# Ten identity products whose results nobody reads, set between TensorE's first and third groups of scores

## The chip, the cores and the metric

The kernel runs on one core of a Trainium2 chip. A core has five engines that work side by side, each through its own list of instructions in order: TensorE (PE, matrix products; its loads of the stationary operand are listed as PEld), VectorE (DVE), ScalarE (ACT), GpSimd (POOL) and SyncE (SP, which here issues the loads and stores). An engine waits for another through semaphores. SBUF holds the operands, PSUM the results of PE, in banks; a PSUM tile of 512 float32 per partition is one bank. The metric is the time of the whole kernel on the device, in microseconds (us), lower is better.

## What is computed

The first part is an attention with a gated state, for 4 batches of 8 heads, 768 steps and heads of 48:

```python
f = 1 / (1 + exp(-f_logit))
for t in range(S):
    state = f[:, :, t, :, None] * state + einsum('bhd,bhe->bhde', k[:, :, t], v[:, :, t])
    y[:, :, t] = einsum('bhd,bhde->bhe', q[:, :, t], state)
```

Its output x (4 x 768 x 384, the heads side by side) goes through a second part:

```python
theta = x @ w_theta
zr, zi = x * cos(theta), x * sin(theta)
u = x + einsum('ts,bsd->btd', w_tok_r, zr) + einsum('ts,bsd->btd', w_tok_i, zi)
return u + maximum(u @ w_ch, 0)
```

## The kernel before

The time axis is cut into chunks of 128 steps, six for each batch, 24 in all; a chunk has two halves of 64. The gates become sums of logarithms, so that a chunk needs no step-by-step recurrence. For chunk m the steps are, by the two letters that the table `ORDER` uses: loads of f, k, q and v (`lf`, `lk`, `lq`, `lv`); the gates on DVE, ACT and POOL (`gc`, `go`, `gs`, `ge`, `gp`), with `gs` a running sum along time (L298, whose first operand `carry` holds 1, and 0 where a chunk begins) and `ge` two exponentials; the scaling of queries and keys (`gq` L313, `gk` L318). PE then has, in small products of 48 or 64 rows and columns, the scores `sc` (L354, keys times queries), the turn of the keys `ke` (L368, four transposes against the identity `ident`), the state sums `up` (L383, turned keys times v), the products with the old state `qs` (L414) and the output `ou` (L422, scores times v). Between them stand copies by other engines: `kt` copies the turned keys (`ktok`), `ma` masks the scores (L360), `sa`, `st` and `sm` form the middle state and the new state on DVE or POOL (L389 to L399), `xc` copies the output to `x`. The turn of x `xt` (L432, three transposes) and the angles `th` (L463, x times w_theta, three products of 128x128 by 384 columns in the first batch) lead to the second part, whose products over time (`f0` to `f2`, L519, tile `pm`) and over channels (`c`, L537) fill most of the run.

Nothing is scheduled by a machine: the table `ORDER` lists the steps of all chunks in one line of words, a loop at the end of the kernel calls them in that order, and each engine gets its instructions in that order. `sc` at its third occurrence is the scores of the third chunk, and so on; `/P`, `/A` or `/D` behind a word puts a step on POOL, ACT or DVE. PSUM has four single banks, tag `b`, and two pairs, tag `a` (the tiles `wide`); `PLACES` says which place each tile takes in turn.

Before the first step the kernel already runs products that nobody reads: 22 of 128x384 from a tile of ones, `seed`, into the bank `b3` (L624 to L629).

Of the kernel before, what the change touches and what calls it, by code (L numbers as in the profile page):

```python
# [75 lines left out]
}  # L76
ORDER = (
# [37 lines left out]
)  # L115


@with_exitstack
def gla_moe_kernel(
# [480 lines left out]
    def group(fn):  # L600
        return lambda n: fn(n // KD, n % KD)
# [165 lines left out]
```

## Time and profile before

| | |
|---|---|
| time, median of 3 runs | 334.77 us (334.46 to 335.71) |
| profiled execution | 335.46 us, its span 333.8 us |
| PE busy | 320.6 us, 96% of the span |
| PE loads / DVE / ACT / POOL busy | 85% / 73% / 57% / 29% |
| mean granted clock of PE | 0.975 |
| read from memory, written | 40.10 MB, 4.72 MB |

The span runs from the first to the last instruction of the program. Busy PE is the time in which a product was in the array by the profile; products are pipelined and their ends are modelled. The granted clock is the share of its full rate that PE was given in a stretch; it is 1.00 or 0.50 here, and a value between means that a stretch saw both. A product of two float32 operands stands in the trace as two records (16 small products as x32), a transpose as one. Times in the rows are counted from the start of the span.

### The profile page before, as it was taken

The page shows a single profiled execution, that of the slowest core. Times are in us where ns is not written, and L with a number is a line of the kernel's source. Part 1 is how long each engine was busy: PE and PEld are TensorE (multiplying, and loading weights), DVE is VectorE, ACT ScalarE, POOL GpSimd, SP SyncE. Part 2 cuts the span into 40 slices and gives each one's busy share as a digit, 9 for nine tenths or more (in the row PEclk, how much of TensorE's full clock was granted, in tenths as well). Part 3 has the DMA queues.
Part 4 walks back from the last instruction along what each step waited for, and adds up shares of the span by engine and source line. Part 5 has one row for each costly group of instructions (what it writes and reads, how often), then busy time and mean ns, then how long its engine had stood idle before and what let it go on. Part 6 is the DMA issues. An engine that isn't in the chain of part 4 may idle for free.

```text
span 333.8 us, 10065 instructions
## 1 busy us (share of the span) xinstructions
PE 320.6 (96%) x4342; PEld 283.4 (85%) x4342; DVE 244.5 (73%) x418; ACT 190.4 (57%) x315; POOL 97.1 (29%) x96
## 2 busy tenths in 40 slices
PE   6689999999999999999999999999999999999993
PEld 6576676566777889999999999999999999999992
DVE  6997999988998977799896667784677476520231
ACT  6787788884778965775766855691363236200010
POOL 3352404024231408516522352321324110132010
PEclk9956999999999999999999999999999999999998
DMA  7988799695604410604444251371102200000012
GB/s 226 379 299 302 227 404 348 244 349 179 224 2 165 152 57 26 217 15 133 139 139 140 81 176 40 105 223 33 48 2 82 73 26 26 0 2 24 24 49 79
DMA packets 21618, 45.54 MB, mean 136 GB/s; under 512 B 2368, under 2 KB 5440, under 8 KB 21568
## 3 DMA queue, kind: packets, MB, share of 16 engines
q1 hardware_dynamic: 21568, 44.83, 39.9%
q8 instruction: 36, 0.59, 0.7%
q14 instruction: 14, 0.11, 0.1%
HBM read 40.10 MB, written 4.72 MB: 134 GB/s over the span
## 4 chain that ended last, share of the span: by engine, by line
PE 93%; DMA 3%; DVE 2%; issue 1%; ACT 1%; SPq 0%; DVEq 0%
PE pm L519 48%; PE pth L463 13%; PE pch L537 11%; PE wide L422 5%; PE wide L414 4%; PE wide L354 4%; PE pxt L432 3%; PE psk L368 3%; PE wide L383 3%; DMA k<-in_k_dram 2%; DMA f<-in_f_dram 1%; DVE f L298 1%; DVE k L318 0%; DVE ut L551 0%; ACT f L294 0%
## 5 line engine op out<-in xcount | busy, mean ns | idle before, releaser
L519 PE MATMUL pm<-wp,z 128*128 128x384 f32 x648 | 119.9, 338 | 0.0
L519 PEld LDWEIGHTS pm<-wp,z 128*128 128x128 f32 x648 | 112.7, 188 | 0.7
L519 PE MATMUL pm<-value,z 128*128 128x384 f32 x144 | 49.8, 488 | 0.0
L537 PE MATMUL pch<-uhl,wch 128*128 128x384 f32 x216 | 42.1, 342 | 0.0
L523 DVE TENSOR_TENSOR ut<-pm,ut 128x384 f32<-128x384 f32 x24 | 13.2, 551 | 36.4 <-PE pm L519 36.2
L519 PEld LDWEIGHTS pm<-value,z 128*128 128x128 f32 x144 | 26.1, 190 | 14.9
L537 PEld LDWEIGHTS pch<-uhl,wch 128*128 128x128 f32 x216 | 37.5, 188 | 0.8
L298 DVE TENSOR_TENSOR_SCAN f<-carry,f 128x512 f32<-128x512 f32 x24 | 29.9, 1250 | 1.7 <-ACT f L294 1.6
L530 POOL TENSOR_TENSOR uhl<-ut,uhl 128x384 fp32r<-128x384 f32 x13 | 14.0, 1078 | 55.1 <-ACT uhl L182 36.2
L288 POOL TENSOR_SCALAR f<-f 128x512 f32<-128x512 f32 x11 | 19.4, 1764 | 20.1 <-DMA f<-in_f_dram 13.3
L454 POOL TENSOR_TENSOR xl<-ut,xh 128x384 fp32r<-128x384 f32 x9 | 10.1, 1125 | 50.7 <-ACT xh L182 23.8
L182 ACT CAST uhl<-ut 128x384 fp32r<-128x384 f32 x13 | 6.7, 512 | 31.9 <-DVE ut L523 31.9
L182 ACT COPY x<-wide 128x384 f32<-128x384 f32 x22 | 10.5, 477 | 24.2 <-PE wide L422 23.1
L463 PE MATMUL pth<-wth,xh 128*128 128x384 f32 x108 | 22.9, 347 | 0.0
L551 DVE SCALAR_TENSOR_TENSOR ut<-pch,ut 128x384 f32<-128x384 f32 x24 | 13.1, 552 | 12.8 <-PE pch L537 12.8
L309 POOL COPY pes<-p 128x4 f32<-128x4 f32 x24 | 8.7, 362 | 46.0 <-ACT p L305 45.1
L503 POOL TENSOR_TENSOR z<-w,z 128x768 fp32r<-128x768 f32 x7 | 13.5, 1927 | 27.6 <-DVE z L182 16.8
L422 PEld LDWEIGHTS wide<-v,sc 64*64 64x64 f32 x768 | 14.9, 138 | 7.2 <-issue 4.1
L318 DVE SCALAR_TENSOR_TENSOR k<-f,k 128x512 f32<-128x512 f32 x24 | 19.2, 801 | 2.2 <-ACT f L306 1.9
L463 PEld LDWEIGHTS pth<-wth,xh 128*128 128x128 f32 x108 | 19.0, 188 | 1.1
L479 ACT ACTIVATE w<-w 128x384 f32<-128x384 f32 x16 | 8.4, 524 | 19.8 <-DVE w L474 19.8
L496 DVE TENSOR_TENSOR w<-w,x 128x768 f32<-128x768 f32 x18 | 18.0, 997 | 2.3 <-ACT w L487 2.3
(88 smaller groups left out, 619.6 us busy)
## 6 DMA issues: line engine op xcount, KB each, us to landing
v<-in_v_dram SPq DMA_DIRECT2D x24, 384.0 KB, 4.8
f<-in_f_dram SPq DMA_DIRECT2D x24, 256.0 KB, 3.8
q<-in_q_dram SPq DMA_DIRECT2D x24, 256.0 KB, 4.7
k<-in_k_dram SPq DMA_DIRECT2D x24, 256.0 KB, 4.9
raw<-in_w_i_dram SPq DMA_DIRECT2D x12, 384.0 KB, 6.2
raw<-in_w_r_dram SPq DMA_DIRECT2D x12, 383.8 KB, 5.6
out_dram<-ut SPq DMA_DIRECT2D x21, 192.0 KB, 2.2
raw<-in_w_theta_dram SPq DMA_DIRECT2D x2, 383.8 KB, 7.0
```

What stands on the lines that cost most here:

```text
L182: (nc.scalar.copy if on(usual) is nc.scalar else on(usual).tensor_copy)(dst, src)
L288: on(nc.vector).tensor_scalar(ft, ft, F_MIN, None, op0=ALU.max)
L298: nc.vector.tensor_tensor_scan(fl, carry[:, pairs(h)].rearrange("p n t -> p (n t)"), fl, 0.0, ALU.mult, ALU.add)
L318: nc.vector.scalar_tensor_tensor(kt, loaded["f", m][:, pairs(h)], E_TOP, kt, op0=ALU.min, op1=ALU.mult)
L354: nc.tensor.matmul(out[HALF[j ^ t], j, p, :], kt[r, p, HALF[t]], qt[r, p, HALF[t]], start=True, stop=True)
L422: nc.tensor.matmul(out[HALF[t], j, p, :], scs[m][HALF[a], j, p, :], v2[HALF[a], t, p, :], start=(t == 0 and m % NC == 0 and p == 0), stop= ...
L463: nc.tensor.matmul(pths[m], l, r, start=(n == 0), stop=(n == len(ms) - 1))
L496: nc.vector.tensor_tensor(zs[m] if full else w, w, xs[m].unsqueeze(1).to_broadcast([P, 2, DM]), op=ALU.mult)
L503: on(nc.vector).tensor_tensor(zs[m][:, 0], ws[m], zs[m][:, 1], op=ALU.subtract)
L519: nc.tensor.matmul(pms[g, d], l, r, start=(s == 0 and i == 0), stop=(s == NC - 1 and i == len(ms) - 1))
L530: on(nc.vector).tensor_tensor(us[g, d][:, 0], uts[g][:, d, :], us[g, d][:, 1], op=ALU.subtract)
L537: nc.tensor.matmul(pcs[g, d], l, r, start=(es[0] == 0 and n == 0), stop=(es[-1] == KD - 1 and n == len(ms) - 1))
```

## The change

A table `WARM` and a step `wm` are added. Each `wm` is one product of the identity (stationary, 128x128) with the first 512 or 256 columns of `carry` (moving), float32 both, into a bank that the table names, `b3` for the first five and `b1` for the rest. No instruction reads the results. `ORDER` gets ten `wm`; apart from these its words and their order are as they were (the lines break elsewhere).

```diff
+WARM = ((512, 3), (512, 3), (512, 3), (512, 3), (512, 3), (256, 1), (256, 1), (512, 1), (256, 1), (256, 1))
+
 ORDER = (
-    "lf lf gc gc go go lf gs gs ge gc/P gp lq lk lq go gk gq lk ge gs ke gq lv lw sc kt up gp lf gk lv ge lk",
+    "lf lf gc gc go go lf gs gs ge gc/P gp lq lk lq go gk gq lk ge gs ke gq lv lw sc kt wm wm up gp lf gk lv",
...
+    def idle_product(i):
+        n, where = WARM[i]
+        none = ps.pool.tile([P, 512], F32, tag=f"b{where}", bufs=1, name=f"none{i}")
+        nc.tensor.matmul(none[:, :n], ident, carry.rearrange("p n t -> p (n t)")[:, :n], start=True, stop=True)
...
-        "f0": piece(0), "f1": piece(1), "f2": piece(2), "v": group(add_u), "uh": group(split_uh), "ul": group(split_ul), "c": channels, "cv": group(finish),
+        "wm": idle_product, "f0": piece(0), "f1": piece(1), "f2": piece(2), "v": group(add_u), "uh": group(split_uh), "ul": group(split_ul), "c": channels, "cv": group(finish),
```

Below is what PE has in a row at three places. In a row stand the line, the operation, the tile that is written, the tiles that are read, and the shape of the result; `wide` are the two pairs of banks, `none` the tiles of the added products. The program after counts its lines 7 higher.

PE before, from the first scores to the third keys' turn:

```order
L354 MATMUL wide_88<-q_141,k_143 64x64 x16
L383 MATMUL wide_89<-v_163,ktok_184 48x48 x16
L368 MATMUL psk_213<-ident,k_151 128x112 x4
L414 MATMUL wide_89<-mid_218,q_141 64x48 x8
L354 MATMUL wide_88<-q_145,k_151 64x64 x16
L383 MATMUL wide_88<-v_206,ktok_254 48x48 x16
L422 MATMUL wide_89<-v_163,sc_220 64x48 x16
L368 MATMUL psk_300<-ident,k_211 128x112 x4
```

PE after, the same stretch:

```order
L361 MATMUL wide_88<-q_141,k_143 64x64 x16
L263 MATMUL none_186<-carry,ident 128x512
L263 MATMUL none_188<-carry,ident 128x512
L390 MATMUL wide_89<-v_163,ktok_184 48x48 x16
L375 MATMUL psk_217<-ident,k_151 128x112 x4
L421 MATMUL wide_89<-mid_222,q_141 64x48 x8
L361 MATMUL wide_88<-q_145,k_151 64x64 x16
L263 MATMUL none_264<-carry,ident 128x512
L263 MATMUL none_266<-carry,ident 128x512
L390 MATMUL wide_88<-v_210,ktok_258 48x48 x16
L429 MATMUL wide_89<-v_163,sc_224 64x48 x16
L263 MATMUL none_308<-carry,ident 128x512
```

Two products of 512 columns stand ahead of the first and of the second state sums, and one behind the first output, ahead of the third keys' turn. The second product of a pair has a wait on PE's own semaphore, for the first one's end.

PE after, from the second chunk's old state to the third's (before, the rows are the same without `none`):

```order
L421 MATMUL wide_89<-st_256,q_145 64x48 x2
L421 MATMUL wide_89<-mid_306,q_145 64x48 x2
L263 MATMUL none_357<-carry,ident 128x256
L263 MATMUL none_359<-carry,ident 128x256
L390 MATMUL wide_88<-v_235,ktok_327 48x48 x16
L263 MATMUL none_383<-carry,ident 128x512
L421 MATMUL wide_88<-st_331,q_262 64x48 x2
```

A pair of 256 columns stands ahead of the third state sums and one of 512 behind them.

PE after, from the second output to the first angles:

```order
L429 MATMUL wide_89<-v_210,sc_318 64x48 x16
L263 MATMUL none_439<-carry,ident 128x256
L375 MATMUL psk_441<-ident,k_336 128x112 x4
L263 MATMUL none_456<-carry,ident 128x256
L361 MATMUL wide_89<-q_262,k_215 64x64 x16
L439 MATMUL pxt_474<-ident,x_430 128x128 x3
L470 MATMUL pth_482<-value_238,ut_446 128x384 x2
```

The last two products of 256 columns stand on either side of the fourth keys' turn; the third scores follow, and from there on PE's list is the old one. The lists of the other engines have the same instructions in the same order as before.

## Rows read from the trace of the kernel before

**Rows 1.** Stretches: length, busy us of each engine (instructions), granted clock, DMA share, GB/s

```profile
14.00:16.00 2.00, 1.16 (x65) 1.07 (x66) 1.58 (x3) 0.62 (x1) 2.00 (x2) 1.00 1.00 384
16.00:18.00 2.00, 1.43 (x11) 0.89 (x14) 1.65 (x3) 1.97 (x5) 1.54 (x3) 0.68 1.02 391
18.00:20.00 2.00, 1.87 (x64) 1.69 (x64) 1.68 (x5) 1.57 (x4) 1.19 (x2) 0.50 1.03 393
...
28.00:30.00 2.00, 2.00 (x6) 0.61 (x4) 2.00 (x4) 0.68 (x2) 0.00 (x0) 0.50 0.80 226
30.00:35.00 5.00, 5.00 (x150) 3.86 (x153) 3.72 (x8) 4.00 (x8) 1.22 (x2) 0.96 0.83 313
...
45.00:50.00 5.00, 5.00 (x140) 3.62 (x139) 4.87 (x8) 3.46 (x8) 0.19 (x1) 1.00 1.05 406
...
100.00:320.00 220.00, 220.00 (x2779) 209.81 (x2778) 150.41 (x249) 113.44 (x184) 64.61 (x57) 1.00 0.26 81
```

**Rows 2.** The chain that ended last, 14 to 40 us: start, length, what

```profile
15.87 0.05 issue
...
18.00 1.23 PE wide L414 x31
...
23.76 0.49 issue
24.25 1.12 PE wide L354 x29
...
26.20 3.84 PE pth L463 x6
...
31.17 0.52 PE wide L354 x32
31.69 0.53 PE psk L368 x4
32.23 0.33 PE pxt L432 x3
32.56 1.94 PE pth L463 x6
34.50 0.61 PE wide L414 x32
...
37.60 0.65 PE wide L422 x32
```

**Rows 3.** PE's timeline: start, length, line, tiles, shapes, records [idle before, released by]

```profile
9.45 0.69 PE L354 MATMUL wide<-q,k 48*64 48x64 f32 x32
11.21 0.58 PE L383 MATMUL wide<-v,ktok 64*48 64x48 f32 x32 [1.06 <-ACT ktok L182]
...
14.64 0.57 PE L383 MATMUL wide<-v,ktok 64*48 64x48 f32 x31 [1.09 <-DMA v<-in_v_dram]
...
15.92 0.60 PE L368 MATMUL psk<-ident,k 112*128 112x112 f32 x4 [0.20 <-DVE k L318]
17.09 0.91 PE L432 MATMUL pxt<-ident,x 128*128 128x128 f32 x3 [0.57 <-ACT x L182]
...
34.93 0.54 PE L383 MATMUL wide<-v,ktok 64*48 64x48 f32 x32
```

**Rows 4.** The page's costliest groups: busy us, mean ns of one record, idle before

```profile
L519 PE MATMUL pm<-value,z 128*128 128x384 f32 x144 | 49.8, 488 | 0.0
```

**Rows 5.** DVE's timeline, columns as in rows 3

```profile
19.92 0.36 DVE L391 TENSOR_TENSOR mid<-wide,st 128x192 f32<-128x192 f32 x1 [0.27 <-PE wide L383]
...
25.49 0.69 DVE L360 TENSOR_TENSOR sc<-wide,causal 128x512 f32<-128x512 f32 x1 [0.55 <-ACT p L305]
...
31.77 0.36 DVE L391 TENSOR_TENSOR mid<-wide,st 128x192 f32<-128x192 f32 x1 [1.06 <-PE wide L354]
32.34 0.69 DVE L313 TENSOR_TENSOR q<-q,p 128x512 f32<-128x512 f32 x1 [0.22 <-ACT p L305]
...
33.22 0.55 DVE L182 COPY ktok<-psk 128x384 f32<-128x384 f32 x1
```

72 rows, old and new, of the table ORDER are left out of this document.

## The prediction

> **What bounds the kernel now.** I read the stretches first, then the chain that ended last, then TensorE's and VectorE's own lines. From 28 us TensorE (PE) is busy for the whole of each stretch that is listed, up to 320 us; VectorE (DVE) is nearly as full from 45 to 50 us, but only 150 of 220 us from 100 on [rows 1]. So a microsecond that the head of the kernel gains or loses on PE should reach the end, unless something else keeps it.
>
> The head is different. The granted clock is 1.00 (2.4 GHz) from 14 to 16 us, averages 0.68 from 16 to 18, is 0.50 (1.2 GHz) from 18 to 20 and still from 28 to 30, and 0.96 from 30 to 35: it falls near 16.7 and comes back just after 30 [rows 1]. What PE did before the fall: groups of small products with two pauses of 1.06 and 1.09 us, at 11.21 behind ScalarE's (ACT) copy of the turned keys and at 14.64 behind a load of v; PE was busy 1.16 us of 14 to 16 and 1.43 of 16 to 18 [rows 1, 3]. What it did before the rise: the three angle products of 128x384, back to back from 26.20 [rows 2]. What the half clock costs is read from pieces of the same work at either rate: the angles 3.84 us and 1.94, the old state 1.23 and 0.61, the turn of x 0.91 and 0.33 [rows 2, 3]. The angles alone give back 1.9 us if the clock stays up.
>
> **The change: what the products cost.** Three angle products of 384 columns take 1.94 us at full clock (they stand as 6 records) and 3.84 us at half [rows 2], so 0.647 and 1.28 us each. The identity and the carries are of the same type and fill the same 128x128, so a product of 512 columns is 0.86 us, one of 256 is 0.43, and at half clock 1.71 and 0.85. All ten (6 of 512, 4 of 256: 4096 columns) are 6.9 us, or 13.7 us at half clock. They are free only as far as they fit into pauses.
>
> Each second product of a pair waits for the end of the first, since both write one bank. No row shows such a wait. A record of such products (384 columns, same type) lasts 488 ns on the mean, and six of them in a row take 1.94, 0.32 us each, so a record has some 0.17 us of tail [rows 2, 4]; from DVE's end at 15.87 to the keys' turn that waited for it at 15.92 is 0.05 us [rows 2, 3]. I take 0.22 us for each of three pairs; the ends are 0 and twice that.
>
> **Walk to the third state sums, if the clock stays full.** The first scores end at 10.14, and PE can take a product from about 10.0. Pair: 0.86 + 0.22 + 0.86 = 1.94, so the first state sums (11.21) start at 11.95, 0.74 late. DVE's first state waits for them, the old-state products wait for that, and the second scores behind them start about 0.6 late and end near 14.15. The second pair runs from 14.0 to 15.95 where 14.64 was: 1.31 late. Those sums and the output take 0.91 (14.64 to about 15.55), then one product of 0.86: the keys' turn starts at 17.7 instead of 15.92 [rows 3]. Here the clock pays back: turn of keys 0.53 (full clock before and after), turn of x 0.33 against 0.91, old state 0.61 against 1.23 [rows 2, 3], so the pair of 256 (0.43 + 0.22 + 0.43 = 1.08) starts at about 19.1 and the third state sums at 20.2. At full clock these take 0.54 with their tail (the row at 34.93) and end near 20.7. DVE's third state starts there instead of at 19.92; I take **0.75 late** [rows 3, 5]. The product behind the sums (0.86) runs while DVE forms that state and costs at most 0.2.
>
> **Then DVE sets the pace.** From 19.92 to 33.77 DVE waits three times: 0.55 at 25.49 (the mask of the third scores; the profile names ACT, but the mask reads these scores, whose last record ends at 24.25 + 1.12 = 25.37 [rows 2]), 1.06 at 31.77 (state sums of the fourth chunk), 0.22 at 32.34 [rows 5]. At full clock PE's old state, output, product, keys, product and scores behind 21.2 take 0.61 + 0.65 + 0.43 + 0.53 + 0.43 + 0.52 = 3.2, and the 0.49 of "issue" that the chain shows at 23.76 may stay [rows 2]: scores at 24.4 to 24.9. DVE comes to the mask at 25.49 - 0.55 + 0.75 = 25.7, so the 0.55 is gone. Turn of x, angles, output and sums (0.33 + 1.94 + 0.65 + 0.54) end by 28.4, and DVE comes for them at 31.77 - 1.06 + 0.75 - 0.55 = 30.9: the 1.06 is gone too. The 0.22 is a wait for ACT's exponential, which stands in ACT's queue behind copies of PE's outputs; I count it as gone, and 0.22 us less if it stays. DVE is then 0.55 + 1.06 + 0.22 - 0.75 = 1.08 earlier at its copy of the fifth keys, which ends 33.77. PE's sums at 34.93 need that copy and had 34.93 - 33.77 - 0.05 = 1.11 to spare [rows 3, 5]. So PE stands there 1.08 + 1.11 = **2.2 us earlier**, at 32.7; its own work (scores 0.52, keys 0.53, turn of x 0.33, angles 1.94, old state 0.61 from 28.4) gets there by 32.4, just before. The last three products cost nothing in this walk, because DVE is the later one from 21 us on; without that cover they would cost their 0.86 + 0.43 + 0.43 = 1.7. With no wait inside the pairs, 0.22 less in each of three, it is 2.9; with twice that wait in each it is 1.5.
>
> Behind 35 us I take the gain as kept, by rows 1. The one thing that could hold it is the loads, since the 16 DMA engines are full from 45 to 50 [rows 1]; 1.0 us is then my lower end, an estimate.
>
> **The sum.** The profiled execution took 335.46 us, its span 333.8 and 1.7 around it. 335.46 - 2.2 = 333.3. It lies 0.69 above the median of the runs shown (334.77, from 334.46 to 335.71); the same step from the median gives 332.6. I say 332.8, nearer to the median, which is what is compared.
>
> **Rivals.** *The clock falls all the same* (slower). The place is 16.7 us: if the stretch from 18 to 20 still shows 0.50, six of the products (2048 columns) run at half rate, 2048/384 x 1.28 = 6.8 us, against later pauses of 1.06 (0.57 and 0.49 [rows 2, 3]). With the 1.31 lost before, PE is 7.0 us late at the angles; those then run in full clock, 1.9 saved, and some 0.6 on the turn of x before them: up to 4.5 us slower, 340.0. The products are as dense as what stood before the rise at 30, so the clock would come back sooner: 337 to 340, middle 338. On a straight line from 2.2 gained (none of the stretch at half clock) to 4.5 lost (all of it), it turns to a loss once a third of the stretch stays at half clock. For it: no pause before the fall is longer than 1.09 us, so the pauses alone may not be the cause. Against: the products put 3.4 us of work like that of 26 to 30 between 10 and 16, and another 3.4 between 17 and 24.
> The Trainium skill ("TensorE: Matmul & The Clock Gate", "Why this matters for your kernels") puts a fall down to idle gaps between bursts, longer ones than any here; by that rule pauses of this length did not cause the fall, filling them brings nothing, and the time would be this rival's. The trace does not agree with the rule as far as it goes: the clock fell with 1.09 us as the longest pause.
>
> *The clock holds at first, falls at one of the leaner places* (old state, sums and scores of 18 to 24 have much small work at full rate) and comes back with the angles: half the gain or a loss of up to 1.5, 333.6 to 336.5.
>
> *It holds, but the gain stays behind*: DVE or the loads keep what PE gained, 1.0 us or less is left, 334.3.
>
> **How the numbers follow.** Forecast (holds, gain 1.5 to 2.9) 0.72; falls all the same 0.10; falls for a part 0.10; gain kept back 0.08. A measurement of this kernel tells about 0.5% (1.7 us) from no change: faster means below 333.1, slower above 336.4. The forecast's range, 331.5 to 334.2, lies on both sides of 333.1; I give two thirds of it to faster, 0.49. Same: 0.23 from the forecast, 0.08 from the gain kept back, 0.06 from the partial fall, 0.37. Slower: 0.10 and 0.04, 0.14. The range of 8 in 10 is 331.6 to 336.0: it leaves out the full fall (0.10), a little of the partial one and the edges of the forecast.
>
> **What would show it.** Right: granted clock 1.00 in every stretch from 18 to 30; products of about 0.86 and 0.43 us; sums at 11.95 and 15.9 where 11.21 and 14.64 stood; DVE's third state late by about 0.7 and its waits at 25.49 and 31.77 gone; PE's fifth state sums near 32.7 instead of 34.93, and the same 2 us at the end. Wrong: 0.50 anywhere in 18 to 28; products of 1.7 us; DVE late by more than 1.5 at the third state; a wait of PE behind 35 us, on a load above all.

## The result: the clock holds, and the kernel is slower

| | before | after |
|---|---|---|
| time, median of 7 runs each, same chip | 334.77 us (334.29 to 335.79) | 336.98 us (336.56 to 337.78) |
| profiled execution, its span | 335.46, 333.8 us | 336.66, 334.9 us |
| mean granted clock | 0.975 | 0.996 |

The ratio is 1.0067, with a 95% interval of 1.0048 to 1.0087: the change costs 0.5 to 0.9%. The forecast was 332.8 us, 331.6 to 336.0. It missed by 4.2 us, on the other side.

The stretches of the kernel after that answer to [rows 1] (same columns: length, busy time of PE, PEld, DVE, ACT, POOL, granted clock, DMA share, GB/s):

```profile
14.00:16.00 2.00, 2.00 (x50) 1.22 (x48) 2.00 (x5) 1.65 (x3) 1.18 (x3) 1.00 1.00 391
16.00:18.00 2.00, 1.94 (x57) 1.02 (x60) 1.03 (x3) 0.00 (x0) 2.00 (x3) 1.00 1.00 375
18.00:20.00 2.00, 2.00 (x34) 1.32 (x25) 2.00 (x4) 0.64 (x2) 0.15 (x1) 1.00 0.96 339
28.00:30.00 2.00, 2.00 (x39) 1.10 (x41) 2.00 (x4) 1.97 (x5) 1.23 (x2) 1.00 1.01 343
30.00:35.00 5.00, 4.76 (x131) 3.30 (x126) 5.00 (x10) 4.27 (x9) 0.81 (x2) 1.00 0.96 305
45.00:50.00 5.00, 4.95 (x139) 3.43 (x138) 4.91 (x9) 3.47 (x8) 0.19 (x1) 1.00 1.04 405
```

The granted clock is 1.00 everywhere, where it was 0.68 and 0.50 from 16 to 30. PE is busy from 14 to 20 almost without a pause. DVE has 1.03 us of work in 16 to 18 where it had 1.65: it waits. What it waits for stands in PE's and DVE's lines of the kernel after (start, length, line, tiles, records, idle before and its releaser), which answer to [rows 3] and [rows 5]:

```profile
9.90 0.69 PE L361 MATMUL wide<-q,k 48*64 48x64 f32 x32
10.52 2.31 PE L263 MATMUL none<-carry,ident 128*128 128x512 f32 x4
12.76 0.58 PE L390 MATMUL wide<-v,ktok 64*48 64x48 f32 x32
...
15.04 2.31 PE L263 MATMUL none<-carry,ident 128*128 128x512 f32 x4
17.28 0.58 PE L390 MATMUL wide<-v,ktok 64*48 64x48 f32 x32
18.29 1.12 PE L263 MATMUL none<-carry,ident 128*128 128x512 f32 x2
19.25 0.55 PE L375 MATMUL psk<-ident,k 112*128 112x112 f32 x4
20.80 1.46 PE L263 MATMUL none<-carry,ident 128*128 128x256 f32 x4
22.18 0.57 PE L390 MATMUL wide<-v,ktok 64*48 64x48 f32 x32
```

```profile
13.40 0.36 DVE L396 COPY mid<-wide 128x192 f32<-128x192 f32 x1 [1.62 <-PE wide L390]
17.99 0.36 DVE L398 TENSOR_TENSOR mid<-wide,st 128x192 f32<-128x192 f32 x1 [0.97 <-PE wide L390]
22.83 0.36 DVE L398 TENSOR_TENSOR mid<-wide,st 128x192 f32<-128x192 f32 x1 [1.77 <-PE wide L390]
...
34.28 0.54 DVE L184 COPY ktok<-psk 128x384 f32<-128x384 f32 x1
```

A pair of 512 columns takes 2.24 us from its start to the start of the state sums behind it (10.52 to 12.76, 15.04 to 17.28), where a pause of about 1.06 stood. The three state sums start at 12.76, 17.28 and 22.18 instead of 11.21, 14.64 and 18.99; DVE waits 1.62, 0.97 and 1.77 us for them and forms the third state 2.9 us late (22.83 for 19.92). Then the waits that DVE had at 25.49, 31.77 and 32.34 are gone, and its copy of the fifth keys is 1.06 late (34.28 for 33.22). The chain that ended last, in the kernel after (start, length, what):

```profile
34.36 0.48 DVE ktok L184
34.88 0.58 PE wide L390 x32
...
48.83 0.48 PE pxt L439 x3
49.30 0.65 PE pm L526 x2
49.95 0.96 issue
50.91 0.81 PE pm L526 x2
```

At 34.88 PE is where it was before at 34.93: the 2.2 us that the forecast gave to the full clock have gone, to the last tenth, into the lateness of the head. Then something new comes: at 49.95 PE stops for 0.96 us between two products of the same kind, and the profile finds nothing that it waits for. From there on it stays about 1.1 us late to the end. The kernel before has no such stop there.

### The profile page after: what moved, and what is told of

Same layout as the page of the kernel before. It is cut to its first block, busy times and chain, and to the rows that moved or that the text cites. A ratio compares the mean times of both kernels' runs of the same rounds, so it can differ in the third digit from the quotient of the medians.

```text
span 334.9 us, 10103 instructions
## 1 busy us (share of the span) xinstructions
PE 324.6 (97%) x4362; PEld 283.8 (85%) x4362; DVE 244.2 (73%) x418; ACT 190.9 (57%) x315; POOL 96.4 (29%) x96
## 4 chain that ended last, share of the span: by engine, by line
PE 91%; DVE 5%; issue 1%; DMA 1%; SPq 0%; DVEq 0%
PE pm L526 48%; PE pch L544 11%; PE pth L470 11%; PE wide L429 4%; PE wide L361 3%; PE wide L421 3%; PE pxt L439 3%; PE psk L375 3%; PE wide L390 3%; PE none L636 2%; DMA raw<-in_w_i_dram 1%; DVE f L305 1%; PE none L263 1%; DVE value L243 1%; DVE k L325 1%
## 5 line engine op out<-in xcount | busy, mean ns | idle before, releaser
L184 ACT COPY x<-wide 128x384 f32<-128x384 f32 x22 | 10.6, 480 | 24.6 <-PE wide L429 23.5
L312 ACT ACTIVATE p<-f 128x512 f32<-128x512 f32 x24 | 15.1, 630 | 8.8 <-DVE q L320 4.7
```

The costliest lines, as they stand in the source:

```text
L184: (nc.scalar.copy if on(usual) is nc.scalar else on(usual).tensor_copy)(dst, src)
L312: nc.scalar.activation(ps_[m][:, pairs(h)], ft, AF.Exp, scale=-1.0)
```

## The experiments

Three theories stood at the start. **Theory 1:** the products hold the clock, and their own length and waits eat what that gives. **Theory 2:** the loss is the stop near 50 us, which comes with the added instructions. **Theory 3:** a held clock brings nothing at all. After the first four runs theory 2 took its final form, on borders between pieces of instructions; it is told there. Theory 1 has two halves: that the length is what hurts, and that a held clock would be worth something without it.

### Size and number of the products

*e1_tiny*, all ten, but 8 columns wide:

```diff
-WARM = ((512, 3), (512, 3), (512, 3), (512, 3), (512, 3), (256, 1), (256, 1), (512, 1), (256, 1), (256, 1))
+WARM = ((8, 3), (8, 3), (8, 3), (8, 3), (8, 3), (8, 1), (8, 1), (8, 1), (8, 1), (8, 1))
```

> All ten products stay, at the same ten places and with the same waits, but each is 8 columns wide instead of 256 or 512: TensorE has the extra instructions and next to none of their array time. Theory 1 (the loss is the products' length: they put the third sums 3.2 us late, against 2.2 us that a held clock gives): the clock falls to 0.5 behind 16 us as in the kernel before, the third sums stand near 19.3 us (18.99 before), and the time is that of the kernel before, 334.3 to 335.3 us, ratio 0.999 to 1.002. Theory 2 (the loss is the pause of about 0.96 us at 50.9 us, which comes with ten more instructions on TensorE whatever their length): a pause of about 1 us stands at the pm product there, and the time is 335.5 to 336.5 us, ratio 1.002 to 1.005. Theory 3 (a held clock brings nothing because VectorE and the loads set the pace): says nothing of this run.

Measured: 337.68 us, ratio 1.0103 (1.0075 to 1.0131), slower than any theory had it. Its stretches and two of its pairs:

```profile
18.00:20.00 2.00, 2.00 (x37) 1.58 (x35) 1.97 (x5) 2.00 (x4) 1.52 (x1) 0.50 1.01 340
28.00:30.00 2.00, 2.00 (x5) 1.09 (x4) 2.00 (x5) 1.97 (x5) 0.00 (x0) 0.50 0.70 241
```

```profile
13.31 0.83 PE L265 MATMUL none<-carry,ident 128*128 128x8 f32 x4
...
19.56 1.25 PE L265 MATMUL none<-carry,ident 128*128 128x8 f32 x4
```

The clock falls as before: the same ten instructions with 8 columns each do not hold it. And a pair of almost no columns still takes 0.83 us, and 1.25 at half clock: the weights are loaded anyway, twice for each float32 product, and the second product waits for the first. Without a held clock to pay for it, DVE's third state starts 1.77 us late (21.69 for 19.92); 0.78 of that is a load of v that landed later, so that the second state sums start at 15.42 instead of 14.64. The run was meant as a control without a cost and isn't one; it says nothing on theory 2, except that a pause of 0.40 us stands before the same pm product as in the kernel after.

*e2_single*, *e3_first* and *e4_last* leave products out (shortened to the widths in `WARM`; a width of 0 means that the product is not issued):

```diff
+e2_single: widths 512, 0, 512, 0, 0, 256, 0, 512, 256, 256
+e3_first:  widths 512, 512, 512, 512, 512, 0, 0, 0, 0, 0
+e4_last:   widths 0, 0, 0, 0, 0, 256, 256, 512, 256, 256
```

> Six of the ten products stay: one of 512 columns where pairs of 512 stood (two places), one of 256 where the pair of 256 stood, one of 512 instead of two in the first five, and the last three as they are. About 4.6 us of product time falls to 3 or so, most of it between the first and the third scores. Theory 1: the clock still holds at 1.00 up to 30 us, the third sums stand at 20.0 to 20.8 us instead of 22.18, VectorE's third state below 21.2 us, and the time is 332.5 to 333.8 us, ratio 0.993 to 0.997. Theory 2: the early part gains the same, but a pause of 1 us at 50 us stays, 333.8 to 334.8 us. Theory 3: the time is 334.5 us or more whatever the third sums show. If the clock falls in spite of the six: 335 to 337 us.

> Only the first five products stay (those up to the third keys' turn); the five behind are out. Theory 1: the clock holds to about 20 us and then falls in the pauses that are open again, the third sums stand about 1.4 us earlier than with all ten, at 20.8 us or so, the scores behind run at half rate for some us: 335 to 337.5 us. Theory 2: the pause at 50 us is gone or moved with five instructions fewer, so about 1 us below the changed kernel, 335.5 to 336 us, whatever the clock does.

> Only the last five products stay (256, 256, 512, 256, 256 columns); the first five, ahead of the third keys' turn, are out. Theory 1: the clock falls behind 16 us as in the kernel before, the first two sums stand as before (11.2 and 14.6 us), the third keys' turn near 15.9 us, the later products run at half rate and twice the length until the clock comes back: third sums at 20.5 to 21.5 us, time 335 to 338 us, ratio 1.001 to 1.010. If the clock holds with these five alone: third sums at 20.5 us and 332.5 to 334 us. Theory 2: 334.3 to 336 us by whether the pause at 50 us is there.

Measured: e2_single 334.42 us, ratio 1.0003 (0.9975 to 1.0030); e3_first 335.53, 1.0046 (1.0005 to 1.0087); e4_last 335.30, 1.0005 (0.9976 to 1.0033). In e2_single the clock holds with six products, DVE's third state is 0.4 us earlier than before instead of 2.9 later, and the kernel is about 0.7% faster than the one with ten (334.42 to 336.98). So the length of the pairs was what hurt, as theory 1 had it (0.46 of the 3.3 us between the two third states are the seeds, which let the first scores start at 9.44 instead of 9.90). But the time stayed 0.6 us above theory 1's range. It lies in that of theory 2, though the stop at 50 us on which that range rested is gone from this run.

Theory 3 asked for 334.5 us or more, which e2_single misses by 0.1; what speaks against it is e4_last, whose ten executions differ in whether the clock held. The three with a mean clock of 0.997 to 0.999 took 333.39 to 333.65 us, the seven with 0.985 to 0.992 took 334.19 to 337.56, 335.6 on the mean: a held clock goes with about 2 us, in one and the same program. This compares executions, not an edit, so what made the clock fall in some of them may have a part in it. Otherwise the two runs decide nothing between theories 1 and 2: e3_first lies in the ranges of both (its third sums start at 20.59, its stop at 50 us is gone, its clock falls at 25.3 us and not near 20), and so does e4_last (its profiled execution loses the clock at 18.3 us, its third sums start at 21.28).

What I take to have kept e2_single from its range is a stop like the one at 50 us, in another place. Here are the stops of e2_single, e3_first and e4_last, in this order:

```profile
20.82 0.68 PE L431 MATMUL wide<-v,sc 64*64 64x48 f32 x32
23.16 0.70 PE L265 MATMUL none<-carry,ident 128*128 128x256 f32 x2 [1.66 <-issue]
```

```profile
22.18 0.66 PE L431 MATMUL wide<-v,sc 64*64 64x48 f32 x29
24.39 0.32 PE L431 MATMUL wide<-v,sc 64*64 64x48 f32 x3 [1.55 <-issue]
```

```profile
18.13 0.26 PE L423 MATMUL wide<-st,q 48*64 48x48 f32 x2 [1.35 <-issue]
```

In e3_first PE stops 1.55 us inside one group of equal products, after 29 records of 32: the profile shows no semaphore that could be the reason. I counted the instructions on PE's list up to each stop (all records that the trace has of PE: products, weight loads, and its few semaphore instructions), and looked for the transfers of PE's instruction queue, which the page lists as `q8 instruction: 36, 0.59, 0.7%`, 36 packets of 16 KB. All pauses of PE of over 0.3 us that end by "issue" in the first 55 us, of the later runs too:

```
kernel        stop ends at  instructions ahead  packet begins  resumed after
before            24.25         705               21.88          2.4
after             50.91         1729              48.51          2.4
e1_tiny           51.38         1729              49.10          2.3
e2_single         17.53         449               15.23          2.3
e2_single         23.16         705               20.51          2.6
e3_first          24.39         705               22.13          2.3
e4_last           18.13         449               15.62          2.5
e5_nowait         24.68         705               22.36          2.3
e5_nowait         50.70         1729              48.15          2.5
e7_before44       18.14         449               15.65          2.5
e8_moved          17.86         449               15.40          2.5
e8_moved          23.74         705               21.32          2.4
e9_after17        52.10         1729              49.58          2.5
e10_moved22       17.98         449               15.67          2.3
e10_moved22       24.20         705               21.62          2.6
e11_four          17.82         449               15.22          2.6
e11_four          23.95         705               21.66          2.3
e12_ahead         24.44         705               21.95          2.5
```

The counts are 449, 705 and 1729 in every kernel: 449 + 256 = 705, and 705 + 4 x 256 = 1729. Whatever stands at those places in the work, a sum, a state, a transpose, the stop is at the border of a piece of 256 instructions, and PE goes on 2.3 to 2.6 us after the packet began. Borders without a stop agree: of all 462 crossings in the 14 traces of this case none comes less than 2.2 us after its packet began. The packet itself began 1.2 to 4.1 us after PE had crossed the border before (18.34 to 21.88 in the kernel before, 46.89 to 48.51 after, 17.84 to 21.95 in e12_ahead). So a piece was usable 3.5 to 6.6 us after the crossing, while 16 products of scores, 64 instructions, run in about 0.5 us at full clock: a stretch of small products uses up a piece before the next is there. This is theory 2 from here on: **PE cannot pass 256 instructions faster than the next piece comes, and the added products move every border behind them.** Why the packet begins late is not tested by an edit, but the traces show what goes with it: of the 462 packets, 105 follow a crossing with the DMA engines over 90% busy in the 2 us behind it, and these begin 2.6 us after the crossing (median); 113 follow one with the engines under 10% busy, and begin 1.4 us ahead of it. The Trainium skill ("Runtime: NRT & Kernel Launch", "Instruction fetch mechanics") says that instructions come in blocks of 16 KiB, 256 instructions, fetched while the block before runs, and that crossing into the next is mostly hidden. The size agrees with the counts; that it is hidden does not hold in this stretch, with stops of 0.4 to 3.2 us.

### The waits inside the pairs

*e5_nowait*: the second product of a pair adds into the first one's tile, and so has no wait for its end (shortened; `...` stands for the moving operand, which is as it was).

```diff
-        none = ps.pool.tile([P, 512], F32, tag=f"b{where}", bufs=1, name=f"none{i}")
-        nc.tensor.matmul(none[:, :n], ident, ..., start=True, stop=True)
+        first = i not in (1, 3, 6)
+        if first:
+            nones[0] = ps.pool.tile([P, 512], F32, tag=f"b{where}", bufs=1, name=f"none{i}")
+        nc.tensor.matmul(nones[0][:, :n], ident, ..., start=first, stop=i not in (0, 2, 5))
```

> All ten products with their columns, but the two of a pair (three pairs) add into one tile instead of writing it one after the other, so that the second has no wait for TensorE's own end of the first. Theory 1 (the products' length): each pair ends 0.2 to 0.3 us earlier than in the changed kernel (2.24 us from the first start to the last end there), the third sums stand 0.6 to 0.9 us earlier than 22.18, and the time falls by that or less: 336.0 to 336.6 us. Theory 2 (TensorE's instructions come in pieces of 256, and what stops it is the arrival of the next piece): the places of the pieces don't move, since the number of instructions is the same; a pause stands at the same pm product near 50 us, longer by what TensorE gained before it: 336.7 to 337.3 us.

Measured: 336.29 us, ratio 1.0036 (1.0019 to 1.0053), 0.7 us below the kernel after and in the range of theory 1, though the intervals of the two ratios overlap.

```profile
10.95 1.98 PE L269 MATMUL none<-carry,ident 128*128 128x512 f32 x4
12.86 0.58 PE L396 MATMUL wide<-v,ktok 64*48 64x48 f32 x32
```

```profile
50.70 0.81 PE L532 MATMUL pm<-value,z 128*128 128x384 f32 x2 [1.14 <-issue]
```

A pair takes 1.91 us to the next start instead of 2.24: the wait costs 0.33 us in each. Both theories have their part: the head is 0.6 us earlier at the third state (with first scores that start 0.42 us later, at 10.32), and the stop near 50 us is longer by 0.2, as theory 2 had it, with a new one of 0.41 at 24.68.

### Moving the borders

More or fewer seed products, with the same columns in total, move every border in the work and change nothing else on PE's list. *e6_after44* does so to the kernel after, *e7_before44* to the kernel before, *e9_after17* to the kernel after in the other direction (there with 17 products of 496 columns):

```diff
-    for _ in range(CONSTANTS):
-        nc.tensor.matmul(none[:, :TH], flat[:, :P], flat[:, P:P + TH], start=True, stop=True)
+    for _ in range(44):
+        nc.tensor.matmul(none[:, :192], flat[:, :P], flat[:, P:P + 192], start=True, stop=True)
```

> The changed kernel with 44 seed products of 192 columns at its start instead of 22 of 384: the same columns, 44 instructions more (a weight load and a product each), so every border between two pieces of 256 instructions moves 44 instructions ahead in the work; nothing else changes. Theory 2: the pause of 0.96 us at the pm product at 50.9 us is gone, since its border now falls among the sums 44 instructions earlier at 48.5 us, 5.7 us behind the border before it; a smaller pause of up to 0.6 us may stand near 18 us; the time falls by 0.5 to 1.0 us against the changed kernel, to 336.0 to 336.5 us. Theory 1 alone: same as the changed kernel, 336.8 to 337.2 us.

> The kernel before, without any of the ten products, and with the same 44 seed products of 192 columns instead of 22 of 384: same columns, 44 instructions more. Theory 2: the borders now fall 44 instructions earlier in the work, two of them where TensorE gets there too soon: pauses ended by nothing the profile shows, of 1 to 1.6 us near 16 to 17 us (among the second sums) and of 1 to 2 us near 49 us (among the states of the sixth chunk), with the first of them perhaps hidden behind the third keys; the time rises by 1 to 2.5 us, to 336 to 337.5 us, though no work was added. Theory 1 alone: same as the kernel before, 334.5 to 335.3 us.

> The changed kernel, with 17 seed products of 496 columns instead of 22 of 384: the same columns within 0.2%, ten instructions fewer, so every border between two pieces of instructions falls ten instructions later in the work, the one near 50.9 us behind the pm product and into the pth products behind it. Theory 2 (borders): the pause of 0.96 us there falls below 0.3 us, a pause of up to 0.5 us may open at the border near 24.7 us, and the time falls by 0.4 to 0.9 us against the changed kernel, to 336.1 to 336.6 us. Theory 1 (length of the products alone): as the changed kernel, 336.8 to 337.2 us.

Measured: e6_after44 337.17 us, ratio 1.0065 (1.0040 to 1.0091); e7_before44 336.59, 1.0055 (1.0030 to 1.0080); e9_after17 336.47, 1.0041 (1.0014 to 1.0067). The first is inconclusive. Its stop at 50 us is gone, as expected, but the 44 narrow seeds took until 10.80 us (9.58 in the kernel after), so the first sums came 1.2 us later, and that ate the gain: columns alone don't give the length of such products. The second shows the mechanism at its clearest. Its lines at the border behind instruction 449:

```profile
14.29 0.63 PE L422 MATMUL wide<-v,sc 64*64 64x48 f32 x26
18.14 0.61 PE L422 MATMUL wide<-v,sc 64*64 64x48 f32 x6 [3.22 <-issue]
```

In the kernel before, with no work added, PE now stops 3.22 us inside one group of sums, at the border that theory 2 named, and the median rises by 1.5 us, inside the expected range (the seeds take until 10.58 here as well, but the first sums come only 0.3 us later for it). What the stop itself costs the trace does not show: the profiled execution is the fastest of the nine, 335.46 us, its third state is 2.15 us late, its fifth keys' copy 0.32, and its end not at all, because DVE's waits took up the rest. The second stop that was expected, near 49 us, did not come: the packet for that border began at 46.53, 0.1 us ahead of the crossing before it, and PE passed at 48.99, 2.46 us after the packet began, without a pause. The third:

```profile
52.10 1.13 PE L472 MATMUL pth<-value,ut 128*128 128x384 f32 x3 [0.55 <-issue]
```

The stop moved with its border, from the second pm product into the pth products behind, and shrank from 0.96 to 0.55 us; below 0.3 had been expected. The time is 0.5 us below the kernel after, inside the expected range, though the two intervals overlap.

### Placing the products against the borders

If PE must wait for a piece anyway, then by theory 2 a product ahead of that border costs nothing, and one behind it costs its full length. *e8_moved* takes e2_single, puts a product of 512 in the place of the one of 256 ahead of the fourth keys' turn, drops the one of 256 behind that turn, and has 19 seeds of 444 columns, so that the product of 512 ends ahead of the border (the widths shortened as above):

```diff
+widths 512, 0, 512, 0, 0, 256, 0, 512, 512, 0
+    for _ in range(19):
+        nc.tensor.matmul(none[:, :444], flat[:, :P], flat[:, P:P + 444], start=True, stop=True)
```

> Five products: 512 columns in the first and in the second pause, 256 ahead of the third sums, 512 behind them, and 512 ahead of the fourth keys' turn; the two of 256 behind the border of the run with six products are out, and the seeds are 19 of 444 columns instead of 22 of 384, which moves the borders six instructions later, so that the last 512 stands ahead of the border, where the run with six products had a pause of 1.62 us. Theory 2: the clock holds, the product of 512 stands in that pause at no cost, the pause shrinks to 0.5 to 1 us, and the time is 0.7 to 1.1 us below the run with six products: 333.3 to 333.8 us. Theory 1 alone (length of the products): about 0.6 us below the run with six, 333.8 us, with no pause of TensorE there.

Measured: 333.71 us, ratio 0.9968 (0.9947 to 0.9988), faster than both kernels.

```profile
21.66 1.12 PE L265 MATMUL none<-carry,ident 128*128 128x512 f32 x2
22.62 0.26 PE L377 MATMUL psk<-ident,k 112*128 112x112 f32 x1
23.74 0.51 PE L377 MATMUL psk<-ident,k 112*128 112x112 f32 x3 [0.86 <-issue]
```

The product stands where the pause was, one transpose follows, and then the border, with 0.86 us left of the stop, inside the 0.5 to 1 expected. The time alone would fit theory 1 as well (333.8); that theory had no stop there. *e10_moved22* is the same with the 22 seeds of 384, *e11_four* the same without the last product:

> The run with five moved products, with 22 seeds of 384 columns as in the kernel before instead of 19 of 444: six instructions more, the work itself the same. Theory 2: the border falls ahead of the last product of 512 again, which then runs behind the pause and not in it: a pause of about 1.6 us ends in front of that product near 23.2 us, the fourth keys' turn starts about 1 us later, and the time is 0.5 to 1.0 us above that run, 334.2 to 334.7 us. Theory 1: the products are the same, so the same time, 333.5 to 333.9 us.

> The run with five moved products without its last one (512 columns ahead of the fourth keys' turn), the seeds 19 of 444 columns as there. Theory 2: that product stood in a pause which TensorE's instructions set anyway, so taking it out makes the pause longer by about 1 us, 1.8 us or so near 22 to 23.7 us, and the time stays within 0.4 us of that run, 333.4 to 334.1 us, if the clock holds over the longer pause; if the clock falls there, 335 to 336 us. Theory 1: one product of 512 less gives 0.5 to 1 us, 332.7 to 333.2 us.

Measured: e10_moved22 335.76 us, ratio 1.0013 (0.9984 to 1.0043); e11_four 334.71, 1.0007 (0.9973 to 1.0041).

```profile
24.20 1.71 PE L265 MATMUL none<-carry,ident 128*128 128x512 f32 x2 [2.26 <-issue]
```

```profile
23.95 0.31 PE L377 MATMUL psk<-ident,k 112*128 112x112 f32 x1 [1.83 <-issue]
```

Six instructions in the seeds decide whether the product runs in the stop or behind it: with the border ahead of it, it starts at 24.20 after 2.26 us of nothing, at half clock (1.71 us), and the median is 2.0 us above e8_moved, twice what was expected. The ten executions show where that comes from: the three with a mean clock of 0.995 to 0.998 took 333.64 to 333.91 us, as long as e8_moved, and the seven with 0.988 to 0.992 took 335.05 to 336.94. Neither group lies in theory 2's 334.2 to 334.7, and three of the ten lie in theory 1's 333.5 to 333.9. So the longer stop shows no cost of its own in these times; the loss goes with the clock, which fell at 24.6 us in the profiled run, 0.4 behind the stop. In e11_four the stop is longer by the product's length, as expected, and the clock fell behind it in the profiled run (0.5 from 25.5 to 28.9 us). Its two executions with a clock of 0.996 and 0.998 took 333.97 and 333.94 us, 0.3 above e8_moved; the other eight, 0.985 to 0.994, took 335.1 on the mean. Both groups lie where theory 2 had them, and theory 1's 332.7 to 333.2 did not come. So the product in the stop costs nothing that these times show, and does have a use.

The stops bear on the clock, then. In the five kernels with a long stop whose profiled run lost the clock behind it, it fell 0.1 to 1.6 us after the stop had ended: e3_first (1.55 us of stop), e4_last (1.35), e7_before44 (3.22), e10_moved22 (2.26) and e11_four (1.83). e2_single and e12_ahead held it over stops of 1.66 and 1.49, so the length of the stop alone does not decide.

*e12_ahead*: the product of 256 ahead of the third sums is out too, and 17 seeds of 496 columns stand for the 19, so that the whole keys' turn comes ahead of the border (shortened as above).

```diff
+widths 512, 0, 512, 0, 0, 0, 0, 512, 512, 0
+    for _ in range(17):
+        nc.tensor.matmul(none[:, :496], flat[:, :P], flat[:, P:P + 496], start=True, stop=True)
```

> Four products of 512 columns (first pause, second pause, behind the third sums, ahead of the fourth keys' turn) without the one of 256, and 17 seeds of 496 columns: eight instructions fewer ahead of the fourth keys' turn than in the run with five moved products, so that the whole turn stands ahead of the border at which that run paused for 0.86 us in the middle of it. Theory 2: the turn runs without a pause, VectorE copies the keys 0.6 to 0.9 us earlier than 24.84 us and, setting the pace from there to 41 us, carries it on: 0.4 to 0.9 us below that run, 332.8 to 333.3 us; the pause of about 1 us stands behind the turn, ahead of the scores. Theory 1: 256 columns less, 0.2 to 0.5 us, 333.2 to 333.5 us, with no change of the pause.

Measured: 333.24 us, ratio 0.9963 (0.9937 to 0.9989), the best of all; next to e8_moved the difference is within the intervals, and both theories' ranges hold this time, so what tells them apart is the place of the stop. Its chain:

```profile
21.31 1.06 PE none L265 x2
22.37 0.39 PE psk L377 x4
22.75 0.20 PE wide L363
22.95 1.49 issue
24.44 0.69 PE wide L363 x31
```

The turn is done in one piece at 22.8, and the stop stands behind it, ahead of the scores. DVE's copy of these keys ends 0.60 us earlier than in e8_moved, as expected; but it was not carried on as expected, for at the fifth keys e12_ahead is 0.25 us behind e8_moved, and what put it 0.56 ahead at the end is not shown. The profiled runs side by side (us against the profiled run of the kernel before; the state's, the copy's and the last channel step's end on DVE):

| | third state | fifth keys' copy | last step | median, us |
|---|---|---|---|---|
| after | +2.90 | +1.06 | +1.10 | 336.98 |
| e5_nowait | +2.31 | +0.48 | +0.97 | 336.29 |
| e9_after17 | +2.87 | +1.05 | +0.92 | 336.47 |
| e2_single | -0.40 | -1.52 | -1.72 | 334.42 |
| e10_moved22, clock lost from 24.6 to 28.0 us | -0.08 | +0.88 | +0.14 | 335.76 |
| e11_four, clock lost from 25.5 to 28.9 us | -0.34 | -1.26 | -1.26 | 334.71 |
| e8_moved | -0.30 | -1.96 | -2.11 | 333.71 |
| e12_ahead | -0.43 | -1.71 | -2.67 | 333.24 |

Where the third state is not late and the clock holds, the gain stands at the fifth keys and reaches the end. The medians show less of it than these profiles, because the profiled run of the kernel before had a clock of 0.975, and 76 other executions of that kernel had 0.975 to 0.994.

## Why the prediction was wrong, step by step

**The clock: right.** It held through every stretch from 18 to 30, with the products as the cause: with their columns taken away (e1_tiny) it fell as before. The rule of the Trainium skill that the prediction weighed ("TensorE: Matmul & The Clock Gate", "Why this matters for your kernels") would have had pauses like those of the kernel before harmless; filling them kept the clock up, and in e11_four it fell with 1.83 us as the longest pause. The slower rival by that rule did not come.

**The worth of the clock: right in size, as far as the runs show it.** 2.2 us at the fifth state sums was forecast for a third state that is 0.75 us late; no run has such a third state, and none holds the clock without added products. In e4_last executions with and without the clock differ by about 2 us, and the profiles of e2_single, e8_moved and e12_ahead end 1.7 to 2.7 us earlier.

**The walk to the third sums: wrong, and this is the step that failed first.** DVE's third state came 2.91 us late instead of 0.75, 2.16 more. Of these, 0.45 are bad luck of the profiled run and not the change: the seeds, the same 22 products ahead of it, take 0.32 us each until the full clock is granted and 0.17 from then on, and that came at 8.30 us here and at 6.47 in the kernel before (6.0 to 9.3 in the others). They ended 0.86 us later (in others at 8.5 to 10.0 us), and put the first scores at 9.90 instead of 9.45. A pair of 512 took 2.24 instead of 1.94, one of 256 1.38 (20.80 to 22.18) instead of 1.08: 0.3 in each of three, 0.9. Two terms were mis-sized: the wait inside a pair, 0.33 us by e5_nowait where 0.22 was taken, and what lies between the last product's columns and the start of the next group, some 0.2 us, where nothing was taken. The single product took 0.96 instead of 0.86. The rest, about 0.7, comes in small pieces: the second scores, which the walk had 0.6 late where the first sums were 0.74 late, came as late as these (1.55 both); from the third keys' turn to the next product it took 1.55 us instead of 1.4; and DVE began 0.65 behind the start of the third sums instead of 0.5.

**DVE sets the pace: right in kind and in size.** The three waits went, as forecast (1.83 us of them), and PE's 1.11 of slack was used. From a third state 2.91 late, the forecast's own sum gives 2.2 - 2.16 = 0.04 us of gain at the fifth sums; measured 0.05 (34.88 for 34.93). The mechanism was right, and the head took all of it. The prediction had named a third state over 1.5 us late as a sign that it was wrong, and that sign came.

**Behind 35 us the gain is kept: wrong.** The forecast looked for a loss there among the loads. It was PE's own instructions: some 40 more on its list (four for each of ten products) moved the border at instruction 1729 into the pm products at 50 us, where the piece was not there yet, 0.96 us. The trace of before had shown the same thing once, 0.49 us of "issue" at 23.76 [rows 2]; the prediction counted it as a cost that might stay, and not as something that moves with the number of instructions.

**The sum.** 2.15 us from the head, 1.15 from the stop and what follows it, 0.5 since the forecast was set below the 333.3 of its own sum towards the median, and 0.3 since the timed runs of the kernel after lie above its profiled one: 4.1 of the 4.2 us by which it missed. The range had no case for a held clock with a loss; its slower rivals all needed a fallen clock.

## What to carry to other kernels

A product that only keeps the clock up must fit into the pause with its weight loads and its wait, not only with its columns: here one product of 512 columns fitted where two did not. And when PE runs many small products, count its instructions: where an "issue" pause stands inside a group of equal products, look whether such pauses lie 256 instructions apart, and try to move the border, or long work ahead of it.

## What the runs showed of the hardware

- PE stops at borders of 256 instructions for 0.36 to 3.22 us when it comes too early, and goes on 2.3 to 2.6 us after the 16 KB packet began (18 stops in 13 kernels; no crossing of 462 earlier than 2.2 us). Before these stops the packet began 1.2 to 4.1 us behind the crossing. Lateness goes with busy DMA engines (2.6 us where they were over 90% busy, 1.4 ahead of the crossing where under 10%, medians); no run changed the loads to test it.
- Six instructions more, far ahead, came with a median 2 us higher (e10_moved22 next to e8_moved), all of it in the seven executions of ten with the lower mean clock; 44 more made the kernel before stop for 3.22 us.
- A pair of float32 products of 8 columns, the second waiting for the first, took 0.83 us at full clock and 1.25 at half; the wait alone cost 0.33 us in a pair of 512.
- One program held its clock in some executions and lost it in others (mean clock 0.985 to 0.999 in e4_last, 0.985 to 0.998 in e11_four), and the times differ by 1 to 2 us with it.
